# A fused attention, routed-expert and squared-gate kernel: raw weight loads are issued a step later in the attention

## The chip, the cores and the metric

The kernel runs on one core of a Trainium2 chip. The metric is the time of one execution on the device in microseconds (us). A core has TensorE (PE: matmuls, and PEld: its weight loads), VectorE (DVE), ScalarE (ACT), GpSimd (POOL) and SyncE (SP, which here only issues transfers and branches). Transfers run on the core's 16 DMA engines; SP, ACT and POOL issue them, each in the order of its own program.

## What is computed

Three layers, one behind the other. The first is attention over 4 batches, 8 heads, 576 positions and 64 features, with a causal window of 64 positions:

```
scores = scale * np.matmul(q, k.transpose(0, 1, 3, 2))
rel = pos[:, None] - pos[None, :]
mask = (rel >= 0) & (rel < window)          # window = 64
scores = np.where(mask, scores, -1000000000.0)
attn = softmax(scores)                       # written out in the reference
return np.matmul(attn, v).astype(np.float32)
```

Its output, 2304 rows of 512, goes through 8 experts (one expert for each row, chosen by the largest of 8 logits; rows with a negative skip score are left as they are): `h = relu(x @ w1[e])`, `y = gate * (h @ w2[e])`, added to x. The last layer is `h = x @ w_in`, a gate made of h and its square, and `g @ w_out`, with 2048 features inside.

## The kernel before

Everything is computed in float32 accuracy with pairs of rounded halves: a weight tile of 512 KB is loaded raw, ACT copies it into the high half (line 131), and another engine subtracts that half from the raw tile to get the low half (line 132). `split_pair` is that pair of operations, called a split here. The weights of the third layer come as 64-bit integers and are converted by DVE first (`convert_ops`).

**Raw places.** Raw tiles live in small pools: 4 places in one, 2 in another during the attention. `to_load` is the list of raw tiles in the order of their use. `load_raws` issues loads on SP as long as fewer than `most[0]` tiles are waiting and a place is free; `most[0]` is 2 + t // 2 in step t. `take_raw` gives a place up in the bookkeeping; a new tile in it still has to wait, in the program, until the split that read the old one has been done. So a load that is issued right behind a split waits, on SP, for that split's subtract.

**The attention.** The loop `for t in range(NT)` (line 578) has 18 steps, one for each 128 rows of the output, written as a pipeline of stages: step t does the scores of tile t (`stage_s`), the transposes of the probabilities of tile t - 2 (`stage_t`, named pt), and the product with the values of tile t - 3 (`stage_v`, named o, line 369), which is the first matmul of a step. So the first o product of the trace is step 3's, and the one at 65.61 us is step 11's. `stage_v` ends with two loads of values, vt, for the next block, into the halves that it has just read (`load_v`, line 299, on SP); they are read two steps later. In odd steps SP also issues q and k of a later block. ACT issues the store of the output tile x (line 387), which has two places. Every third step has routing work (`route_a`, `route_b`, `route_h` on POOL, `route_c`), which makes a number for each row by which the experts gather their rows.

At the end of a step stands one split, on ACT and POOL, if the raw tile has been known for two steps:

```
            if splits and since.get(splits[0][1:], t) + 2 <= t:
                work(splits, [pool])
            if t:
                load_raws()
```

`work` calls `do_split`, which calls `load_raws` itself behind the split. Beside it, from step 6 on, the operations of two conversions are spread over the steps (`convert_by_parts`), and this too calls `load_raws` when a conversion is done. Behind the loop comes the drain: the last stages, the last routing, and then the gathers for the first expert. In the experts and in the last layer splits, conversions and loads are called in other places, by the same functions.

Of the kernel before, what the change touches and what calls it, by code (L numbers as in the profile page):

```python
# [64 lines left out]
def moe_chain(  # L65
# [26 lines left out]
    pool, dve = nc.gpsimd, nc.vector  # L92
# [3 lines left out]
    def load_raws(eng=nc.sync):  # L96
        while to_load and len(raws) < most[0]:
            used = [n for _, n in raws.values()]

            last = to_load[0] in LATE  # L100
            room = [n for n in range(1 if last else len(rawp)) if used.count(n) < RAWS[n]]
            if not room:
                return
            u, c = to_load.pop(0)

            n = min(reversed(room), key=lambda n: left.get(n, 0))
            at = rawp[n]
            if u < U_IN:
                r = at.tile([P, 2, 512], F32, tag="raw", name=f"raw{u}_{c}")
                eng.dma_start(r, wu[u, :, c : c + 2])  # L110
            else:
                r = at.tile([P, 512, 2], I32, tag="raw", name=f"raw{u}_{c}")
                eng.dma_start(
                    r.rearrange("p n w -> p (n w)").bitcast(I64), wd[u - U_IN, :, c]
                )
            raws[u, c] = r, n
# [3 lines left out]
    def take_raw(key):  # L120
        r, n = raws.pop(key)
        left[n] = max(left.values(), default=0) + 1
        return r
# [5 lines left out]
    def split_pair(u, c, src, into, eng):  # L129
        t = into.tile([P, 2, 2, 512], F32R, tag="pair", name=f"w{u}_{c}")  # L130
        nc.scalar.activation(t[:, 0], src, AF.Copy)  # L131
        eng.tensor_tensor(t[:, 1], src, t[:, 0].bitcast(F32), ALU.subtract)  # L132
        halves[u, c] = t[:, :, 0]
        halves[u, c + 1] = t[:, :, 1]

    def convert_ops(w, r, mag=None):

        low, high = r[:, :, 0], r[:, :, 1]  # L140
        wf = w.bitcast(F32)
        v = nc.vector
        ops = [
            partial(
                v.tensor_scalar, w, high, 3, 0x3FFFFFFF, op0=ALU.logical_shift_left, op1=ALU.bitwise_and
            ),
            partial(
                v.scalar_tensor_tensor, w, high, -0x40000000, w, op0=ALU.bitwise_and, op1=ALU.bitwise_or
            ),
            partial(  # L150
                v.scalar_tensor_tensor, w, low, 29, w, op0=ALU.logical_shift_right, op1=ALU.bitwise_or
            ),
        ]
        if mag is None:
            ops.append(partial(v.tensor_single_scalar, high, high, 0x7FFFFFFF, ALU.bitwise_and))
            mag = high.bitcast(F32)
        ops.append(partial(v.scalar_tensor_tensor, wf, mag, LEAST, wf, op0=ALU.is_ge, op1=ALU.mult))
        return ops

    def convert(w, r):  # L160
        for op in convert_ops(w, r):
            op()

    def do_split(u, c, eng):
        split_pair(u, c, take_raw((u, c)) if u < U_IN else early.pop((u, c)), ring, eng)
        load_raws()

    def do_convert(u, c, into):
        if c % 2 == 0:
            early[u, c] = into.tile([P, 2, 512], F32, tag="early", name=f"c{u}_{c}")  # L170
        convert(early[u, c // 2 * 2][:, c % 2].bitcast(I32), take_raw((u, c)))
        load_raws()

    def convert_by_parts(todo, into):

        for _, u, c in todo:
            if c % 2 == 0:
                early[u, c] = into.tile([P, 2, 512], F32, tag="early", name=f"c{u}_{c}")
            for op in convert_ops(early[u, c // 2 * 2][:, c % 2].bitcast(I32), raws[u, c][0]):
                yield  # L180
                op()
            take_raw((u, c))
            load_raws()

    def work(todo, engines):

        for eng in engines[: len(todo)]:
            what, u, c = todo.pop(0)
            if what == "s":
                do_split(u, c, eng)  # L190
            else:
                do_convert(u, c, early_pool[0])
# [75 lines left out]
    with ExitStack() as actx:  # L268
# [40 lines left out]
        def scale_q(i):  # L309

            if i < NBLK:
                nc.scalar.activation(qt[i], qt[i], AF.Copy, scale=SCALE)
# [49 lines left out]
        def stage_v(t):  # L362
            o = psp.tile([P, H, P], F32, tag="o", name=f"o{t}")

            pts = [st.pop(("pt", 2 * t + k)) for k in range(2)]
            for h in range(H):
                for k in range(2):
                    half = (h + k) % 2
                    nc.tensor.matmul(  # L369
                        o[k * BLK : (k + 1) * BLK, h, 0:VW],  # L370
                        lhsT=pts[k][:, h // 2, half * BLK : (half + 1) * BLK],
                        rhs=vt[(2 * t + k) % B][:, h * VW : (h + 1) * VW],
                        start=True, stop=True,
                    )
            den = sm.tile([P, H, 1], F32, tag="den", name=f"den{t}")
            nc.vector.tensor_scalar_add(den, o[:, :, D : D + 1], 1e-9)
            rec = sm.tile([P, H, 1], F32, tag="rec", name=f"rec{t}")
            nc.vector.reciprocal(rec, den)
            x = ap2.tile([P, H, D], F32, tag="x", name=f"x{t}")
            nc.vector.tensor_tensor(x, o[:, :, 0:D], rec.to_broadcast([P, H, D]), ALU.mult)  # L380
            st["x", t] = x.rearrange("p h d -> p (h d)")
            i, b = divmod(2 * t, B)
            load_v(i + 1, b)
            load_v(i + 1, b + 1)
# [32 lines left out]
        def keep_warm(n):  # L417
            spare = psp.tile([P, P], F32, tag="o", name="spare")
            for _ in range(n):
                nc.tensor.matmul(spare, lhsT=ones, rhs=ones, start=True, stop=True)  # L420
# [108 lines left out]
        def route_c(t, n):  # L529

            ix = misc[:, 128 : 128 + NE * NT]

            last = t + n == NT
            near = not last and t + 2 * n >= NT
            for i in reversed(range(n)):
                to, at = st.pop(("to", t + i))
                nc.tensor.matmul(
                    ix, lhsT=to, rhs=at, start=(not last and i == n - 1), stop=(not near and i == 0)
                )
            if last:  # L540
                keep_warm(KEEP[2])
            if not near:
                nc.vector.tensor_tensor(idx if last else acc, ix, acc, ALU.add)
            if last:
                nc.vector.tensor_tensor(cnt_i, st.pop("cn"), base[:, 0], ALU.subtract)


        splits = [("s", p // 2, p % 2 * 2) for p in range(RING)]
# [27 lines left out]
        due, since = {}, {}  # L576
        parts = convert_by_parts(converts, earlyp)
        for t in range(NT):
            if t >= 3:
                stage_v(t - 3)  # L580
            if t >= 2:
                stage_t(t - 2)
            if t % 2:
                scale_q(t // 2 + 1)
            stage_s(t)
            most[0] = 2 + t // 2
            if t % 2:
                load_q(t // 2 + 2)
                load_k(t // 2 + 3)
            if t >= 3:  # L590
                store_t(t - 3, nc.scalar)
            if t >= 6:
                next(parts, None)
            if t >= 5:
                stage_l2(t - 5, *of[t - 5][1:])
            if t >= 4:
                stage_l(t - 4)
            if t >= 3:
                stage_x(t - 3)
            if t >= 5:  # L600
                t0, i, n, side = of[t - 5]
                if i == n - 1:
                    route_a(t0, n)
                    for f, l in (
                        (partial(route_b, t0, n, side), 1),
                        (partial(route_h, t0, n), 2),
                        (partial(route_c, t0, n), 4),
                    ):
                        due.setdefault(t + l, []).append(f)
            for f in due.pop(t, ()):  # L610
                f()
            if t >= 6:
                next(parts, None)

            if splits and since.get(splits[0][1:], t) + 2 <= t:
                work(splits, [pool])
            if t:
                load_raws()
            for key in raws:
                since.setdefault(key, t)  # L620

        t1, n = NT - ROUTES[-1], ROUTES[-1]
        t0 = t1 - ROUTES[-2]
# [33 lines left out]
        route_h(t1, n)  # L657
        route_c(t0, of[t0][2])
        route_c(t1, n)
        for _ in parts:  # L660
            pass
        work(splits, [pool] * len(splits))
# [445 lines left out]
```

## Time and profile before

| | |
|---|---|
| median of the runs shown | 731.54 us (731.29 to 736.42, 3 runs) |
| the profiled execution | 736.77 us, with a span of 735.0 us from the first to the last instruction |
| PE, PEld busy | 684.8 us (93%), 582.6 us (79%) |
| DVE, ACT, POOL busy | 431.6 us (59%), 382.9 us (52%), 94.6 us (13%) |
| mean granted TensorE clock | 0.975 of full speed |
| a split: copy on ACT, subtract on POOL | 1058 ns, 2360 ns (means) |
| loads of raw tiles | 62 of 512 KB from the experts' weights and 32 of the last layer's on SP |

The profile is of one execution. PE's busy time is that of pipelined matmuls, with modelled ends, so a busy PE can still be slow: the granted clock has two levels, 1.2 and 2.4 GHz, and a mean share below 1 says how much of a stretch ran at the lower. The loop of the attention ends at about 116 us, the drain at 145 us. The timeline gives for each group of instructions its start, its duration, engine, line, operation, tiles and, in brackets, the idle time in front of it with what ended it.

### The profile page before, as it was taken

How to read it: one execution, taken by the hardware profiler on the slowest of the kernel's cores; microseconds unless marked ns; L12 is line 12 of the kernel's file. 1: busy time of each engine (PE TensorE's matmuls, PEld its weight loads, DVE VectorE, ACT ScalarE, POOL GpSimd, SP SyncE). 2: the span in 40 equal slices, each digit the busy share in tenths (PEclk: the TensorE clock that was granted, in tenths of full speed). 3: DMA queues.
4: the chain of work that ended last, by engine and by line, in shares of the span. 5: the costliest groups of instructions: out<-in, count | busy, mean ns of one | idle time of the engine just before them, and what ended most of it. 6: DMA issues, size and time to landing. Idle time of an engine off the chain costs nothing.

```text
span 735.0 us, 12186 instructions
## 1 busy us (share of the span) xinstructions
PE 684.8 (93%) x4605; PEld 582.6 (79%) x4605; DVE 431.6 (59%) x852; ACT 382.9 (52%) x760; POOL 94.6 (13%) x96
## 2 busy tenths in 40 slices
PE   7987887798999999899999999999999999999997
PEld 6765666676777777488789899999989989999985
DVE  4678776458759268968788884434433333343332
ACT  5756561026556266456666665545444454455443
POOL 2336662402112112200000000000000000000000
PEclk9999998789999999999999999999999999999999
DMA  7998954248859349453233400303030020001002
GB/s 255 310 304 250 253 175 117 61 136 279 291 172 347 130 146 293 132 181 122 94 109 107 125 6 1 71 15 73 16 86 1 1 68 19 1 1 43 1 1 43
DMA packets 34502, 88.81 MB, mean 121 GB/s; under 512 B 6958, under 2 KB 8110, under 8 KB 34420
## 3 DMA queue, kind: packets, MB, share of 16 engines
q1 hardware_dynamic: 26352, 74.60, 33.5%
q10 hardware_dynamic: 5748, 6.57, 2.9%
q0 software_dynamic: 2320, 6.58, 2.9%
q8 instruction: 47, 0.77, 0.4%
q14 instruction: 35, 0.29, 0.1%
HBM read 75.65 MB, written 13.12 MB: 121 GB/s over the span
## 4 chain that ended last, share of the span: by engine, by line
PE 52%; DVE 4%; ACT 1%; DMA 1%; issue 1%; SPq 0%; ACTq 0%; DVEq 0%
PE h L865 25%; PE po L893 25%; PE p2x L855 1%; DVE c L886 1%; DMA x<-x 1%; DVE c_first L992 1%; DVE c L883 1%; ACT q L876 1%; DVE w L132 0%; DVE gs L884 0%; DVE q L875 0%; DVE x2T L127 0%; ACT q L872 0%; DVE q L879 0%; ACT part L902 0%
## 5 line engine op out<-in xcount | busy, mean ns | idle before, releaser
L865 PE MATMUL h<-x2T,w 128*128 128x384 f32 x1152 | 218.1, 337 | 1.0 <-DVE x2T L127 0.9
L893 PE MATMUL po<-w,gs 128*128 128x512 f32 x864 | 217.3, 395 | 1.6 <-ACT w L131 0.9
L865 PEld LDWEIGHTS h<-x2T,w 128*128 128x128 f32 x1152 | 204.6, 188 | 10.1 <-DVE x2T L127 1.7
L893 PEld LDWEIGHTS po<-w,gs 128*128 128x128 f32 x864 | 159.5, 188 | 32.2 <-ACT w L131 1.2
L872 ACT ACTIVATE q<-h 128x384 f32<-128x384 f32 x96 | 47.0, 490 | 108.4 <-PE h L865 106.8
L875 DVE TENSOR_SCALAR q<-q 128x384 f32<-128x384 f32 x96 | 34.3, 358 | 98.2 <-ACT q L872 98.1
L879 DVE TENSOR_TENSOR q<-hs,q 128x384 f32<-128x384 f32 x96 | 53.6, 559 | 49.8 <-ACT q L876 49.8
L881 ACT ACTIVATE gs<-q 128x384 fp32r<-128x384 f32 x96 | 50.4, 525 | 60.0 <-DVE q L879 60.0
L884 DVE TENSOR_TENSOR gs<-q,gs 128x384 fp32r<-128x384 f32 x96 | 53.6, 559 | 44.4 <-ACT gs L881 44.4
L131 ACT ACTIVATE w<-raw 128x1024 fp32r<-128x1024 f32 x64 | 65.3, 1058 | 19.1 <-PEq L808 6.4
L748 PE MATMUL y<-w,hT 128*128 128x512 f32 x264 | 70.9, 404 | 4.6 <-DVE hT L127 3.7
L748 PEld LDWEIGHTS y<-w,hT 128*128 128x128 f32 x264 | 47.4, 188 | 18.5 <-DVE hT L127 6.7
L876 ACT ACTIVATE q<-q 128x384 f32<-128x384 f32 x96 | 50.5, 526 | 22.0 <-DVE q L875 18.4
L132 DVE TENSOR_TENSOR w<-raw,w 128x1024 fp32r<-128x1024 f32 x50 | 59.0, 1220 | 3.9 <-ACT w L131 2.2
L343 ACT ACTIVATE pr<-s,nb 128x128 f32<-128x128 f32 x144 | 39.2, 383 | 23.0 <-DVE nb L339 23.0
L874 ACT ACTIVATE hs<-h 128x384 f32<-128x384 f32 x96 | 46.8, 488 | 0.0
L710 PE MATMUL ha<-w,mxT 128*128 128x512 f32 x132 | 35.5, 421 | 6.9 <-PEq L808 4.1
L132 POOL TENSOR_TENSOR w<-raw,w 128x1024 fp32r<-128x1024 f32 x14 | 33.0, 2360 | 57.7 <-ACT w L131 57.7
L710 PEld LDWEIGHTS ha<-w,mxT 128*128 128x128 f32 x132 | 25.7, 201 | 16.1 <-issue 9.5
L369 PE MATMUL o<-vt,pts 128*64 128x65 f32 x576 | 26.5, 247 | 9.5 <-DMA vt<-in_vs 8.0
L710 PE MATMUL hb<-w,mxT 128*128 128x512 f32 x132 | 35.2, 402 | 0.0
L127 DVE TENSOR_TENSOR hT<-hTp,hT 128x512 fp32r<-128x512 f32 x22 | 15.1, 688 | 32.4 <-ACT hT L126 27.2
(164 smaller groups left out, 708.9 us busy)
## 6 DMA issues: line engine op xcount, KB each, us to landing
raw<-in_wu SPq DMA_DIRECT2D x62, 512.0 KB, 5.3
raw<-in_wd SPq DMA_DIRECT2D x32, 512.0 KB, 3.8
x<-x SPq DMA_DIRECT2D x21, 256.0 KB, 3.7
vt<-in_vs SPq DMA_DIRECT2D x36, 130.0 KB, 6.3
x<-x ACTq DMA_DIRECT2D x18, 256.0 KB, 6.5
out<-out SPq DMA_DIRECT2D x36, 128.0 KB, 2.4
q<-in_qs SPq DMA_DIRECT2D x8, 512.0 KB, 5.7
kt<-in_ks SPq DMA_DIRECT2D x8, 512.0 KB, 6.4
```

Of the source, the lines that this page charges most:

```text
L131: nc.scalar.activation(t[:, 0], src, AF.Copy)
L132: eng.tensor_tensor(t[:, 1], src, t[:, 0].bitcast(F32), ALU.subtract)
L710: nc.tensor.matmul(ph, lhsT=xT[:, a, c, :], rhs=halves[4 * e + j, c][:, b, :], start=(n == 0), stop=(n == len(seq) - 1),)
L748: nc.tensor.matmul(py, lhsT=hT[j][:, a, c, :], rhs=halves[4 * e + 2 + j, c][:, b, :], start=(j == 0 and c == 0 and (a, b) == PASSES[0]), s ...
L865: nc.tensor.matmul(ph, lhsT=halves[U_IN + m // 4, c][:, b, (m % 4) * P : (m % 4 + 1) * P], rhs=xT[:, a, c, :], start=(n == 0), stop=(n == ...
L872: nc.scalar.activation(q, ph, AF.Relu, bias=0.5, scale=0.5)
L874: nc.scalar.activation(h, ph, AF.Copy)
L876: nc.scalar.activation(q, q, AF.Square)
L879: nc.vector.tensor_tensor(q, h, q, ALU.max)
L881: nc.scalar.activation(gs[:, 0], q, AF.Copy)
L884: dve.tensor_tensor(gs[:, 1], q, gs[:, 0].bitcast(F32), ALU.subtract)
L893: nc.tensor.matmul(po[i], lhsT=gs[:, a, i * P : (i + 1) * P], rhs=w[:, b, :], start=(m == m0 and (a, b) == PASSES[0]), stop=(m == m1 - 1 a ...
```

## The change

Two things. First, in the attention neither a split nor a conversion calls `load_raws` any more: a flag, `at_once`, is false until the drain's last statement, where it is set and `load_raws` is called once. From there on everything is called as before. Second, at the end of a step `load_raws` and the note in which step a tile came (`since`) now stand ahead of the split instead of behind it.

```diff
+    at_once = [False]
+
     def do_split(u, c, eng):
         split_pair(u, c, take_raw((u, c)) if u < U_IN else early.pop((u, c)), ring, eng)
-        load_raws()
+        if at_once[0]:
+            load_raws()
...
             take_raw((u, c))
-            load_raws()
+            if at_once[0]:
+                load_raws()
...
-            if splits and since.get(splits[0][1:], t) + 2 <= t:
-                work(splits, [pool])
             if t:
                 load_raws()
             for key in raws:
                 since.setdefault(key, t)
+
+            if splits and since.get(splits[0][1:], t) + 2 <= t:
+                work(splits, [pool])
...
         route_c(t1, n)
+        at_once[0] = True
+        load_raws()
         for _ in parts:
             pass
```

PE and DVE keep every instruction in its order. SP, ACT and POOL change in the attention and the drain alone. A raw tile is named by its unit and column (raw6_2), and w6_2 is its split; the last number is a running one. On SP from step 11's loads of q and k to the end of step 13, before:

```order
L290 DMA q7_1284<-in_qs 128x1024
L294 DMA kt_148<-in_ks 128x1024
L110 DMA raw6_2_1289<-in_wu 128x1024
L113 DMA raw32_2_1336<-in_wd 128x512
L299 DMA vt2_151<-in_vs 64x520
L299 DMA vt3_152<-in_vs 64x520
L113 DMA raw32_3_1441<-in_wd 128x512
L299 DMA vt0_149<-in_vs 64x520
L299 DMA vt1_150<-in_vs 64x520
L290 DMA q8_1517<-in_qs 128x1024
L110 DMA raw7_0_1554<-in_wu 128x1024
```

The same place in the changed kernel:

```order
L295 DMA q7_1277<-in_qs 128x1024
L299 DMA kt_148<-in_ks 128x1024
L110 DMA raw5_2_1324<-in_wu 128x1024
L110 DMA raw6_0_1326<-in_wu 128x1024
L304 DMA vt2_151<-in_vs 64x520
L304 DMA vt3_152<-in_vs 64x520
L110 DMA raw6_2_1431<-in_wu 128x1024
L304 DMA vt0_149<-in_vs 64x520
L304 DMA vt1_150<-in_vs 64x520
L295 DMA q8_1510<-in_qs 128x1024
L113 DMA raw32_2_1544<-in_wd 128x512
```

The pattern stays, two vt loads and one raw load for each step, but the raw tiles come later: raw6_2 moves from step 11 to 12, raw32_2 from step 11 to 13, raw7_0 from 13 to 15. The last of the attention, raw8_0, moves from step 16 to the end of the drain, behind the last store of x. Before, raw32_2 takes the place of raw4_0, which is split in the same step 11; now it takes the same place in step 13, and raw4_0 is split in step 12.

On ACT the splits' copies move one step: there is none in step 7, and the last, w6_2, moves from step 16 to step 17. The end of the loop on ACT, before (pr are the exponentials, x14 and gate9 stores of rows and gates, pts34 belongs to the drain):

```order
L456 ACTIVATE ex9_1886<-d9_1875 128x24
L131 ACTIVATE w6_2_1888<-raw6_2_1289 128x1024
L357 ACTIVATE pts30_1923<-pt30_1918 128x512
L343 ACTIVATE pr34_1956<-s34_1932,nb34_1952 128x128 x4
L343 ACTIVATE pr35_1961<-s35_1933,nb35_1954 128x128 x4
L387 DMA x1_68<-x14_1914 128x512
L507 DMA x1_68<-gate9_1995 128x3x1
L357 ACTIVATE pts34_2061<-pt34_2056 128x512
```

and in the changed kernel:

```order
L461 ACTIVATE ex9_1879<-d9_1868 128x24
L131 ACTIVATE w6_0_1883<-raw6_0_1326 128x1024
L362 ACTIVATE pts30_1916<-pt30_1911 128x512
L348 ACTIVATE pr34_1949<-s34_1925,nb34_1945 128x128 x4
L348 ACTIVATE pr35_1954<-s35_1926,nb35_1947 128x128 x4
L392 DMA x1_68<-x14_1907 128x512
L512 DMA x1_68<-gate9_1988 128x3x1
L131 ACTIVATE w6_2_2004<-raw6_2_1431 128x1024
L362 ACTIVATE pts34_2059<-pt34_2054 128x512
```

w6_2's copy now stands behind the gate's store and ahead of pts34. On POOL its subtract stands, as before, ahead of the six operations of `route_h` for rows 9 to 11, but it too is of step 17 now.

## Rows read from the trace of the kernel before

**Rows 1.** Stretches: duration, busy us (count) of each engine, clock, DMA share, GB/s.

```profile
16.00:44.00 28.00, 25.51 (x432) 19.80 (x428) 18.68 (x40) 20.32 (x54) 9.46 (x4) 0.95 1.03 313
65.60:87.00 21.40, 17.20 (x271) 13.18 (x271) 17.83 (x58) 13.99 (x35) 11.29 (x9) 0.92 0.88 266
```

**Rows 2.** PE's waits, 16 to 117: us in total, times, longest us.

```profile
PE o L369 <- DMA vt<-in_vs: 8.0, 7, 2.6
...
PE o L369 <- DVE oh L452: 1.4, 1, 1.4
...
PE px L393 <- DVE x L380: 0.6, 1, 0.6
```

**Rows 3.** PE's timeline: start, duration, instruction, count, [idle before it].

```profile
65.61 1.69 PE L369 MATMUL o<-vt,pts 128*64 128x65 f32 x32 [1.76 <-DMA vt<-in_vs]
67.23 1.97 PE L353 MATMUL pt<-ident,pr 128*128 128x128 f32 x8
...
74.69 1.16 PE L369 MATMUL o<-vt,pts 128*64 128x65 f32 x32
...
79.52 1.15 PE L369 MATMUL o<-vt,pts 128*64 128x65 f32 x32
80.61 1.09 PE L353 MATMUL pt<-ident,pr 128*128 128x128 f32 x8
...
87.06 0.33 PE L369 MATMUL o<-vt,pts 128*64 128x65 f32 x2 [2.63 <-DMA vt<-in_vs]
87.56 1.97 PE L369 MATMUL o<-vt,pts 128*64 128x65 f32 x30 [0.17 <-DMA vt<-in_vs]
89.45 1.66 PE L353 MATMUL pt<-ident,pr 128*128 128x128 f32 x8
...
106.09 0.33 PE L369 MATMUL o<-vt,pts 128*64 128x65 f32 x2 [0.92 <-DMA vt<-in_vs]
107.81 1.97 PE L369 MATMUL o<-vt,pts 128*64 128x65 f32 x30 [1.38 <-DVE oh L452]
109.70 1.77 PE L353 MATMUL pt<-ident,pr 128*128 128x128 f32 x8
```

**Rows 4.** Waits of SP's queue, 16 to 120: us in total, times, longest us.

```profile
SPq L110 <- POOL w L132: 20.3, 6, 8.0
SPq L113 <- POOL w L132: 14.0, 3, 4.9
...
SPq L299 <- DMA x<-x: 5.8, 3, 3.5
```

**Rows 5.** SP's timeline: start, duration of the issue, transfer, count.

```profile
58.78 1.11 SPq L299 DMA_DIRECT2D vt<-in_vs  x2
...
79.85 0.33 SPq L113 DMA_DIRECT2D raw<-in_wd  x1
80.27 1.13 SPq L299 DMA_DIRECT2D vt<-in_vs  x2
...
100.60 0.33 SPq L110 DMA_DIRECT2D raw<-in_wu  x1
101.03 1.11 SPq L299 DMA_DIRECT2D vt<-in_vs  x2
```

**Rows 6.** POOL's timeline, the subtract of step 11's split.

```profile
77.46 2.37 POOL L132 TENSOR_TENSOR w<-raw,w 128x1024 fp32r<-128x1024 f32 x1 [6.61 <-ACT w L131]
```

**Rows 7.** Issues, 16 to 117: transfer, count, KB each, median us to landing.

```profile
vt<-in_vs SPq DMA_DIRECT2D x30, 130.0 KB, 6.5
x<-x ACTq DMA_DIRECT2D x15, 256.0 KB, 8.7
```

**Rows 8.** Timelines of POOL, ACT and PE in the drain.

```profile
121.60 0.85 POOL L523 TENSOR_SCALAR at<-slot_c,rc,val 128x144 fp32r<-128x144 f32 x1
...
122.11 0.60 ACT L357 ACTIVATE pts<-pt 128x512 f32<-128x512 f32 x1 [6.16 <-PE o L369]
...
128.99 0.89 PE L537 MATMUL misc<-at,to 128*128 128x144 f32 x3 [1.10 <-DVE mine L439]
```

## The prediction

> **What bounds the kernel now.** I read the stretches first, then PE's waits, then PE's timeline step by step, then the SP queue and POOL. The change lies in the attention, the first 116.7 us of a 735.0 us span, with a drain behind it until the first expert starts. The later two thirds are TensorE work in which no instruction moves, so they only start earlier or later.
>
> In the attention PE should be the pace: a plain step, from one o product to the next, is 4.83 us (74.69 to 79.52 [rows 3]). But PE's longest wait there is for vt, the values of a block: 8.0 us in seven waits, and one more of 1.4 put down to DVE that is of the same kind, 9.4 in all [rows 2]. (I read the 1.4 as vt too: o does not use oh, and the pair's second DMA, issued half a microsecond behind the one at 101.03, would land about then.) Step by step: 1.76 us in step 11 (o at 65.61), 2.63 + 0.17 in step 14 (87.06, 87.56), 0.92 + 1.38 in step 17 (106.09, 107.81) [rows 3]; that is 6.86, and the other 2.5 lie in steps 6 and 8.
>
> Each of these three idle times is followed by slower matmuls. The eight transposes pt take 1.09 us at full clock (80.61), but 1.97, 1.66 and 1.77 behind the three stalls; o takes 1.15 (79.52), but 1.69 and twice 1.97 [rows 3]. In both stretches shown the mean granted clock is below 1: 0.95 and 0.92 [rows 1]. So a stall costs its idle time and then (0.54 + 0.88), (0.82 + 0.57) and (0.82 + 0.68) us in o and pt, 4.3 together; other instructions that fall into it I leave out.
>
> Why is vt late? A pair of vt loads may go out as soon as the o product that reads its place is done, and is needed two steps later. In step 12 that o ends at 74.69 + 1.16 = 75.85 [rows 3], but SP issues the pair at 80.27, right behind a raw load at 79.85 [rows 5]. That raw load wants the place that step 11's split gave up, and POOL's subtract of that split ends at 77.46 + 2.37 = 79.83 [rows 6]. SP works in order, so the pair sits 4.4 us behind a load that nobody needs yet. The same shows at 100.60 and 101.03 for step 17, and the pair at 58.78 for step 11 goes out behind three raw loads [rows 5]. Over the attention SP waits 20.3 + 14.0 us in nine such cases [rows 4].
>
> **The change part by part.** (1) The raw load moves out of the split. At the end of a step SP now asks for a place freed in an earlier step. Call L the time from the o product of a step to the end of that step's subtract. For step 12 the pair was held until L of step 11 had run out, one step after that o; now the wait for that subtract stands in front of step 13's pair, one whole step later. Step 11's subtract ends at 79.83, step 13's o at 79.52 + 1.15 = 80.67: the wait is over before the pair is released. At worst, where two plain steps follow each other and POOL has its six routing operations ahead of the subtract, I expect under 1 us of it to be left, and a pair has two plain steps less its o, 2 x 4.83 - 1.15 = 8.5 us, to land; the median landing is 6.5 [rows 7], so 2.0 us are in hand. The stalls of steps 14 and 17 then go: 2.80 + 2.30. For step 11, the pair stands behind one raw load that waits for a conversion, not three, so most of 1.76 goes; I take all of it and put the doubt into the deduction below. With the half-speed stretches behind them, 6.86 + 4.3 = 11.2 us.
>
> (2) Fewer raw bytes ahead. The splits from w2_0 on come one step later (no split in step 7, w6_2 in step 17), and each raw load behind them mostly two steps later. From 16 to 44 us the DMA engines are full (share 1.03, 313 GB/s [rows 1]), and the vt pair of step 8 stands behind one raw load fewer: 512 KB at 313 GB/s is 1.7 us. The stalls of steps 6 and 8 sum to 2.5; I take 1.7. Bounds: nothing, if what is ahead is replaced by something else, and 2.5 plus one more slow stretch of 1.4.
>
> The Trainium skill ("DMA: Bandwidth & Descriptors", Specifications) gives about 358 GB/s as what one core gets from HBM; the stretch at 313 agrees as an upper limit. By the page's figure 512 KB would be 1.5 us, and the sum would fall by 0.2.
>
> (3) What comes next in its place. From 65.6 to 87.0 the DMA engines are busy 0.88 of 21.4 us, 18.8 us of work [rows 1]. Without step 11's slow stretch (1.42) and step 14's idle (2.80) PE would want it done in 17.2. So up to 1.6 us comes back as later landings; nothing, if the slack from (2) covers it. The output tile x has two places and its store lands in 8.7 us at the median [rows 7] against 9.7 for two plain steps, so DVE and then the transposes of x can be held: PE has 0.6 of that now, once [rows 2]. I take 0.6 to 1.2. I deduct 2.9 in all: 1.6 for the DMA work, 0.9 for x, 0.4 for step 11.
>
> (4) The drain. w6_2's copy (ACT) and subtract (POOL) now stand at the end of step 17. ACT has 6.16 us idle in front of pts at 122.11, and the copy takes about 1 us. POOL's six routing operations end at 121.60 + 0.85 = 122.45; 2.4 us later is 124.8, and the product that reads them starts at 128.99, behind DVE [rows 8]. So nothing, with 4 us of cover on POOL; if the cover were gone, up to 2.4. raw8_0 moves behind the last x store on SP, where SP has only the read of the counts left. No cost.
>
> Sum: 11.2 + 1.7 - 2.9 = 10.0 us. The profiled execution took 736.77 us, 5.2 above the median of 731.54; I cannot see where those 5.2 lie. Since the mechanism is in the order of the program, I take the gain as it is: 736.8 - 10.0 = 726.8 for such an execution, **721.5 us** for the median. If part of the 5.2 were in these very stalls, the median would gain less.
>
> **The rivals.** A is the forecast: the three stalls behind raw loads go, a gain of 7.4 to 15.5 (15.1 is 11.2 + 2.5 + 1.4 without deduction), 716 to 724.1.
>
> B: the DMA engines take over. vt goes out earlier but lands later, since a cycle of three steps has about as many bytes as before, and part of the stalls returns with its slow stretches. For it: a share of 0.88 to 1.03 up to 87 us [rows 1], and vt pairs that already wait for an earlier store's completion, 5.8 us in three cases [rows 4]. Against: only 0.88 in the stretch with the 2.8 us stall, and every raw load stands later. If two of the three slow stretches stay (2.9) and a third of the idle time (2.3), the gain is 10.0 - 5.2 = 4.8: 726.7, with 725 to 731 around it. The Trainium skill ("DMA: Bandwidth & Descriptors", Issuing engines are not separate DMA queues) says that the sequencer's own time is usually small beside the DMA itself; taken alone that speaks for B, but here it is not the issue of 0.33 us that holds the pair, it is the wait in front of it.
>
> C, slower: nothing holds SP back any more, so vt pairs go out into a fuller queue and land late everywhere. It decides from a landing of 8.5 us on. At 11 us each two-step round is 2.5 short: in the three routing cycles from step 9 to 17, two rounds of each, 6 x 2.5 = 15 us of idle time, with a slow stretch of 1.4 for each cycle 19, against the 11.2 that go: 8 us slower, 739.5. Against it: raw loads in flight are limited by free places, and now fewer are in flight; the median is 6.5 [rows 7].
>
> D, the change does not do what it says: the subtract is so late that the raw load still holds the next pair. It needs L above two steps, 9.7 us and more, by as much as now. L is 79.83 - (65.61 + 1.69) = 12.5 for step 11, but the two steps behind it take 13.4 (o from 65.61 + 1.69 to 80.67). Then within 1 us of 731.5.
>
> **How the numbers follow.** A 0.62, B 0.28, C 0.04, D 0.06. One per cent of 731.5 is 7.3 us, about what a measurement of this kernel can tell from no change, so A is faster (0.62), B and D are within 1% (0.34), C is slower (0.04). The range 716.0 to 730.0 holds A, and of B and D most of B; it leaves out some 0.04 below, 0.12 above. For A alone 716 to 724.
>
> **What would show it.** In the changed kernel: SP's waits for POOL w fall from 34 us to little, or no longer stand ahead of a late vt pair; PE's wait for vt falls from 9.4 to under 3; pt stays near 1.1 us in steps 11, 14 and 17; the last o product of the loop starts about 10 us earlier; everything from the first expert on is shifted, not changed. I am wrong in (1) if vt pairs still go out 4 us behind their o, in (3) if they go out in time and PE still waits with DMA at 1.0 (B) or for x, and in (4) if the distance from the last o to the first gather grows.

## The result, and the profile after

The changed kernel takes 725.23 us (median of 4) beside 733.98 us of the kernel before (median of 4): ratio 0.9873, 95% interval 0.9824 to 0.9923. Run once more beside other kernels it gave 0.9877 (0.9836 to 0.9919). Single executions of one kernel lie up to 14 us apart, and as a rule those with a higher granted clock are the shorter ones, so small differences are read from many executions and not from one. Ratios and means leave out executions that were more than 1.5% above the kernel's shortest.

The profiled execution has a span of 723.6 us, 11.4 less than before. From TensorE's timeline, the starts of the o products:

| from … to | before, us | after, us | less by |
|---|---|---|---|
| step 3's o: start | 16.08 | 17.25 | -1.2 |
| step 3 to 9 | 36.92 | 33.31 | 3.6 |
| step 9 to 11 (ends with step 11's stall) | 12.61 | 10.84 | 1.8 |
| step 11 | 9.08 | 9.33 | -0.3 |
| step 12 | 4.83 | 6.08 | -1.3 |
| step 13 to 15 (step 14's stall) | 15.91 | 11.33 | 4.6 |
| step 15 to 17 | 10.66 | 9.67 | 1.0 |
| step 17 | 10.62 | 7.83 | 2.8 |
| first o of the drain to the first expert's transposes | 28.57 | 27.83 | 0.7 |
| from there to the end of the span | 589.7 | 590.1 | -0.4 |

So the gain is made in the attention, and the rest is shifted, not changed. The first row is no gain or loss of the change: up to there the instructions are the same. One profile stands behind each column, and single rows vary: in a second profile of the changed kernel (span 724.2 us) the first expert starts 9.4 us earlier than before, not 11.8. The attention of the profile before is not an unusual one: its first expert starts at 145.28 us, and that of the kernel below that changes the order alone, and gains nothing, at 146.09.

TensorE's waits after, 16 to 117 us (us in total, times, longest), as [rows 2]:

```profile
PE pt L358 <- DVE xT L400: 4.5, 6, 1.4
PE misc L542 <- DVE ls L419: 2.1, 2, 1.2
PE px L398 <- DVE x L385: 1.6, 3, 0.6
...
PE o L374 <- DMA vt<-in_vs: 0.5, 1, 0.5
```

The wait for values, 9.4 us before, is 0.5 us. What leads now are waits for DVE's copies (xT, ls), each 1.4 us or less. SyncE's queue, 16 to 120 us, as [rows 4]:

```profile
SPq L304 <- PE o L374: 15.8, 8, 5.5
SPq L110 <- POOL w L132: 10.9, 4, 4.6
SPq L113 <- POOL w L132: 5.7, 3, 2.6
```

The waits for POOL's subtract are halved, 34.3 to 16.6 us, not gone; but SyncE now waits most for the o product itself, which is when the pair of vt should go out. The timeline of steps 12 to 14, as [rows 5]:

```profile
72.76 1.11 SPq L304 DMA_DIRECT2D vt<-in_vs  x2
75.89 0.33 SPq L110 DMA_DIRECT2D raw<-in_wu  x1
77.99 1.12 SPq L304 DMA_DIRECT2D vt<-in_vs  x2
80.60 0.33 SPq L295 DMA_DIRECT2D q<-in_qs  x1
82.48 0.33 SPq L113 DMA_DIRECT2D raw<-in_wd  x1
82.92 1.40 SPq L304 DMA_DIRECT2D vt<-in_vs  x2
```

and TensorE's, as [rows 3]:

```profile
62.23 1.12 PE L374 MATMUL o<-vt,pts 128*64 128x65 f32 x30 [0.50 <-DMA vt<-in_vs]
64.53 1.09 PE L358 MATMUL pt<-ident,pr 128*128 128x128 f32 x8 [1.18 <-DVE xT L400]
...
69.54 0.53 PE L542 MATMUL misc<-at,to 128*128 128x144 f32 x3 [1.19 <-DVE ls L419]
70.54 0.18 PE L471 MATMUL misc<-oh,stri 128*128 128x27 bf16 x1 [0.47 <-DVE acc L548]
...
70.73 2.00 PE L374 MATMUL o<-vt,pts 128*64 128x65 f32 x32
72.67 1.49 PE L358 MATMUL pt<-ident,pr 128*128 128x128 f32 x8
...
76.81 1.15 PE L374 MATMUL o<-vt,pts 128*64 128x65 f32 x32
...
81.65 1.16 PE L374 MATMUL o<-vt,pts 128*64 128x65 f32 x32
82.73 1.09 PE L358 MATMUL pt<-ident,pr 128*128 128x128 f32 x8
...
97.81 1.15 PE L374 MATMUL o<-vt,pts 128*64 128x65 f32 x32
98.89 1.09 PE L358 MATMUL pt<-ident,pr 128*128 128x128 f32 x8
```

In step 12 the o product ends at 70.73 + 2.00 = 72.73 and its pair of vt goes out at 72.76; in step 13 at 77.96 and 77.99. Before, step 12's pair stood 4.4 us behind. Steps 14 and 17 (o at 81.65 and 97.81) have no stall and run o and pt at full speed. From step 4 to the end of the loop only step 12 has slow ones (2.00 and 1.49), behind step 11's waits. Of these, the ones for ls and acc stood there before too, and then step 12 ran at full speed; new in step 11 are 0.50 us for vt and 1.18 for xT. Before:

```profile
73.51 0.53 PE L537 MATMUL misc<-at,to 128*128 128x144 f32 x3 [1.09 <-DVE ls L414]
74.50 0.17 PE L466 MATMUL misc<-oh,stri 128*128 128x27 bf16 x1 [0.47 <-DVE acc L543]
```

The stretches and landings after, as [rows 1] and [rows 7]:

```profile
16.00:44.00 28.00, 26.51 (x488) 20.80 (x480) 18.92 (x41) 21.05 (x57) 9.48 (x4) 0.95 1.00 316
65.60:87.00 21.40, 19.30 (x320) 14.89 (x317) 18.00 (x55) 14.80 (x39) 13.68 (x10) 0.92 1.01 297
```

```profile
vt<-in_vs SPq DMA_DIRECT2D x32, 130.0 KB, 6.3
x<-x ACTq DMA_DIRECT2D x15, 256.0 KB, 7.3
```

The DMA engines are busier from 65.6 to 87 us (share 1.01, before 0.88), because the attention passes sooner, and the values land 6.3 us after issue at the median, as before. That median, like the 6.5 of [rows 7], is of few loads: the profile holds the landings of 8 of the 32 (5 of the 30 before). The second profile of the changed kernel has 28 of them, with a median of 6.9 and 9.0 us at the longest.

### The profile page after: what moved, and what is told of

Read it like the earlier page. It is cut to its first block, busy times and chain, and to the rows that moved or that the text cites. A ratio compares the mean times of both kernels' runs of the same rounds, so it can differ in the third digit from the quotient of the medians.

```text
span 723.6 us, 12188 instructions
## 1 busy us (share of the span) xinstructions
PE 678.7 (94%) x4605; PEld 578.4 (80%) x4605; DVE 430.5 (59%) x852; ACT 382.7 (53%) x760; POOL 93.6 (13%) x96
## 4 chain that ended last, share of the span: by engine, by line
PE 49%; DVE 7%; ACT 2%; issue 1%; DMA 0%; ACTq 0%; DVEq 0%; SPq 0%
PE po L901 24%; PE h L873 24%; DVE c L894 2%; ACT q L884 1%; PE p2x L863 1%; DVE gs L892 1%; DVE c L891 1%; DVE w L132 1%; DVE c_first L1000 1%; DVE q L883 1%; DVE q L887 1%; DVE x2T L127 0%; DMA x<-x 0%; ACT q L880 0%; PE spare L989 0%
## 5 line engine op out<-in xcount | busy, mean ns | idle before, releaser
L127 DVE TENSOR_TENSOR hT<-hTp,hT 128x512 fp32r<-128x512 f32 x22 | 15.1, 688 | 33.1 <-ACT hT L126 25.4
L344 DVE TENSOR_REDUCE nb<-s 128x4 f32<-128x512 f32 x36 | 23.1, 684 | 13.4 <-PE s L337 8.5
```

## The experiments

Three kernels stand around the change: is it the wait on SyncE, or the order of the bytes?

**The order alone.** From the kernel before:

```diff
-            if splits and since.get(splits[0][1:], t) + 2 <= t:
-                work(splits, [pool])
             if t:
                 load_raws()
             for key in raws:
                 since.setdefault(key, t)
+            if splits and since.get(splits[0][1:], t) + 2 <= t:
+                work(splits, [pool])
```

> The kernel before, with the raw load of the free places written ahead of the split, but the split and the conversion still load at once into the place they leave. On SP each raw load from the eighth step on now stands one pair of value tiles later than before, as it does after the change; but each one still needs the place of the split made in the same step, so SP still stops there. If the wait counts (the theory of the forecast): SP's idle time for POOL's w stays near the 34 us of before (25 to 40), the o product still waits for vt about three times, and the time is within 0.4% of before (ratio 0.996 to 1.004). If it is the order of the bytes on the DMA engines that counts (raw bytes behind the value tiles and not ahead of them): ratio 0.985 to 0.99, as after the change.

Measured: ratio 0.9997 (0.9968 to 1.0025). The waits, of TensorE and of SyncE's queue:

```profile
PE o L369 <- DMA vt<-in_vs: 9.0, 6, 2.3
```

```profile
SPq L110 <- POOL w L132: 29.2, 7, 8.8
SPq L113 <- POOL w L132: 7.6, 3, 4.9
```

36.8 us on SyncE and 9.0 on TensorE, as before. Later raw bytes alone bring nothing.

**A spare place.** From the kernel before, splits and loads where they were:

```diff
-            most[0] = 2 + t // 2
+            most[0] = min(2 + t // 2, 5)
...
         route_c(t1, n)
+        most[0] = 1 + NT // 2
+        load_raws()
```

> The kernel before, split and loads in their old places, but at most five of the raw places are filled in the attention loop, so that a place stays spare and a load that follows a split takes the place left by an earlier one. If the wait counts: SP's idle time for POOL's w falls under 15 us, the o product's waits for vt are gone (under 2 us in place of 8.0), and the ratio is 0.985 to 0.99, as after the change. If the step's place in the code (the raw load beside the branch, one step later) is what counts, and not the wait: ratio 0.996 to 1.004.

Measured: 0.9885 (0.9849 to 0.9922). The same two views:

```profile
PE o L369 <- DMA vt<-in_vs: 1.8, 2, 1.4
```

```profile
SPq L113 <- POOL w L132: 7.8, 3, 3.1
...
SPq L110 <- POOL w L132: 5.3, 3, 1.9
```

With the calls where they were, the gain comes once the wait falls (13.1 us). What the change moved is one way to it, not the thing itself.

**Another queue.** From the kernel before, with a flag, `on_pool`, that is true around the loop's split alone:

```diff
     def do_split(u, c, eng):
         ...
-        load_raws()
+        load_raws(pool if on_pool[0] else nc.sync)
```

> The kernel before, but in the attention loop the raw load that follows a split is issued by POOL, which has just made the split, and no longer by SP. The load goes out at the same moment as before, with the same bytes ahead of the same value tiles; only SP no longer stops for it. If the wait on SP counts: the o product's waits for vt go from 8.0 us to under 2.5, the half-clock stretches at steps 11, 14 and 17 go, and the ratio is 0.985 to 0.992 (a little less gain than after the change, by the 1.7 us that the raw bytes ahead of step 8's value tiles cost and what POOL spends to issue). If the DMA engines and not the queue hold the value tiles (rival B, or the order of the bytes): ratio 0.995 to 1.003. If issuing from POOL itself is dear: POOL is late with the next w and the ratio is above 1.0.

Measured: 0.991 (0.9879 to 0.9942).

```profile
PE o L371 <- DMA vt<-in_vs: 0.6, 2, 0.4
```

```profile
SPq L110 <- POOL w L132: 4.1, 1, 4.1
```

Up to 51 us the raw loads go out 3 to 8 us later than before, but from 57 to 90 us within 1 us of their old times (79.65, 87.14 and 90.40 us; before 79.85, 86.42 and 89.68), and the waits for vt of steps 14 and 17 are gone all the same. They also go over another DMA queue here, so this run alone doesn't tell SyncE's wait from the place of the raw bytes ahead of the values in one queue; the spare place does, where they stay on SyncE's. The three together show that the cause was the in-order wait on SyncE. The Trainium skill ("DMA: Bandwidth & Descriptors", Issuing engines are not separate DMA queues) says that issuing on several engines saves only the sequencer's time, usually small beside the DMA; for the 0.33 us of an issue that holds here, but not for a wait in front of it, which cost about 1% of this kernel.

**Filling the wait.** Is it TensorE's waiting that brings the half-clock stretches behind it? From the kernel before:

```diff
             if t >= 3:
+                if t in (11, 14, 17):
+                    keep_warm({11: 24, 14: 36, 17: 14}[t])
                 stage_v(t - 3)
```

> The kernel before, with idle-time matmuls of ones (results unused) ahead of the o product in steps 11, 14 and 17: 24, 36 and 14 of them, which at 62 ns each fill 1.5, 2.25 and 0.87 us of the 1.76, 2.63 and 0.92 us that TensorE waits there for value tiles. The waits for POOL on SP and the arrival of the value tiles stay as they are. If TensorE's waiting is what brings the half-clock stretches behind it (the forecast's 4.3 us of its 11.2): the granted clock at 66.8, 87.3 and 107.7 us is no longer half, the o and pt of these steps run at 1.15 and 1.1 us again, and the time falls by 2.5 to 4.3 us (ratio 0.994 to 0.997). If the stretches come whatever TensorE does there: ratio 0.999 to 1.003 and the stretches stand where they stood.

Measured: 1.006 (1.0024 to 1.0095), slower, where 0.994 to 0.997 was expected. Yet in its profile the three slow stretches are gone (pt of steps 11, 14 and 17 takes 1.09 us, at a granted clock of 1.00) and the first expert starts at 138.03 us, 7.2 before its old place; then the experts and the last layer take 596.5 us instead of 589.7. That difference stands in TensorE's waits at the branches for second tiles (136 to 290 us), first of the kernel before, then of this one:

```profile
PE ha L710 <- PEq L808: 4.1, 2, 2.8
```

```profile
PE ha L712 <- PEq L810: 11.4, 5, 3.9
```

The wait is of TensorE's own sequencer, behind the branch; the 74 matmuls and their weight loads had made the program in front longer. The clock fell there too: from the first expert to 290 us it is 0.96 here and 0.98 before, while up to the first expert it is 0.95 and 0.91. So the next kernel has as many instructions as before; `keep_warm_wide` issues matmuls of 512 columns, with the same ones:

```diff
-                    keep_warm({11: 24, 14: 36, 17: 14}[t])
+                    keep_warm_wide({11: 7, 14: 10, 17: 4}[t])
...
-        for _ in range(WARM):
+        for _ in range(WARM - 28):
             nc.tensor.matmul(warm, lhsT=ones, rhs=ones, start=True, stop=True)
+        keep_warm_wide(7)
```

> The kernel before with TensorE's waits for value tiles filled as in the run with the idle-time matmuls, but with matmuls of 512 columns (7, 10 and 4 of them, results unused, about the same 1.5, 2.2 and 0.9 us), and 28 of the 58 warm-up matmuls ahead of the attention put together to 7 wide ones, so that TensorE has just as many instructions as before and the code behind the attention lies where it lay. That run ended its attention 7.2 us earlier than the kernel before, and lost 6.8 us in the experts, where TensorE's sequencer stood idle at the branches for second tiles for 11.4 us in place of 4.1. If that loss came from where the added code put the branches: the first expert starts at 138 to 140 us as there, the experts take the 590 us of before, and the time is 4 to 7 us less than before (ratio 0.990 to 0.995). If the loss comes from the attention's end being moved at all, or the half-clock stretches only went elsewhere: ratio 0.998 to 1.006.

Measured: 0.9984 (0.995 to 1.0019). The sequencer's wait is back at its old size:

```profile
PE ha L719 <- PEq L817: 4.3, 2, 3.0
```

and the three stretches that ran at half clock before (columns as in [rows 1], the clock is the third number from the end), first before, then here:

```profile
66.80:70.20 3.40, 3.40 (x24) 2.38 (x24) 3.01 (x14) 2.71 (x4) 1.72 (x1) 0.50 0.96 350
87.30:90.70 3.40, 3.23 (x38) 3.05 (x37) 1.06 (x3) 0.03 (x1) 2.35 (x1) 0.51 0.92 245
107.70:111.10 3.40, 3.29 (x37) 3.20 (x38) 1.06 (x4) 0.45 (x2) 2.36 (x1) 0.50 0.79 203
```

```profile
66.80:70.20 3.40, 3.14 (x52) 2.07 (x50) 3.17 (x8) 2.53 (x6) 2.37 (x1) 1.00 0.78 274
87.30:90.70 3.40, 3.40 (x55) 2.34 (x53) 2.54 (x5) 1.01 (x3) 1.46 (x1) 1.00 0.97 206
107.70:111.10 3.40, 2.77 (x49) 2.10 (x50) 2.46 (x6) 1.58 (x7) 0.00 (x0) 1.00 0.93 246
```

All three are at 2.4 GHz. But step 12, which ran at full speed before, now has a slow o and pt:

```profile
72.20 1.67 PE L369 MATMUL o<-vt,pts 128*64 128x65 f32 x32
73.80 1.97 PE L353 MATMUL pt<-ident,pr 128*128 128x128 f32 x8
```

So two of the three stretches went, and one came a step later. And the gain of 4 to 7 us did not come, though this profile's first expert starts at 140.42 us, 4.9 before its old place: the interval allows at most 3.7 and none at all. Each execution's span and mean granted clock say what became of it. Take span x (1 - clock) as the time not granted: 17.4 us over 21 executions of the kernel before, 13.6 over 12 of this one, 3.8 less (standard error 1.5). The remainder of the span grew from 716.6 to 718.7 us, by 2.1 (standard error 1.1). So filling brings part of the clock back, and about half of that seems to be paid for again by the fill itself, presumably where the values come before it ends. The run before this one does not show it in its executions: 16.8 us not granted over 11, beside 16.2 over 16 of the kernel before. That its loss in the experts came from where the longer code put the branches is what the pair suggests; an earlier end of the attention alone does not bring it, since the kernel after, whose first expert starts earlier still, waits 4.0 us there. What exactly the sequencer waits for isn't settled.

**What comes next after the change.** Now from the kernel after; first that kernel itself, once more:

> The changed kernel once more, beside the others on the same chip: ratio 0.985 to 0.991 to the kernel before, 724 to 727 us.

Measured: 0.9877 (0.9836 to 0.9919).

```diff
             for f in due.pop(t, ()):
                 f()
-            if t >= 6:
+            if t >= 6 and t != 9:
                 next(parts, None)
```

> The kernel after, with the conversion's eighth of ten DVE operations moved from the end of step 9 to the beginning of step 10's group (the ninth and tenth follow one place later), so that it no longer stands beside POOL's subtract. If DVE, held 1.5 us by that subtract, took the place of the value tiles in step 11 (the term of the forecast that did not come): the operation takes 0.7 us in place of 2.2, TensorE's waits for xT and ls around 62 to 70 us fall by 1 to 2 us, the half-clock stretch at 70 us goes, and the time is 1 to 3 us under the kernel after (ratio to before 0.983 to 0.987). If DVE's lateness there has other causes or another wait stands right behind it: the ratio is that of the kernel after within 0.1%.

Measured: 0.9871 (0.9825 to 0.9917), no difference to the kernel after that these six executions can resolve; the 1 to 3 us expected are within the interval. The rows tell why there is little to see. DVE's operation and POOL's subtract at that place, in the profile after, in the second one of the same kernel, and here:

```profile
61.46 2.22 DVE L185 SCALAR_TENSOR_TENSOR c<-raw,c 128x512 int32<-128x512 int32 x1
...
60.78 2.35 POOL L132 TENSOR_TENSOR w<-raw,w 128x1024 fp32r<-128x1024 f32 x1
```

```profile
63.62 0.69 DVE L185 SCALAR_TENSOR_TENSOR c<-raw,c 128x512 int32<-128x512 int32 x1
...
60.57 2.35 POOL L132 TENSOR_TENSOR w<-raw,w 128x1024 fp32r<-128x1024 f32 x1
```

```profile
61.27 1.70 DVE L185 SCALAR_TENSOR_TENSOR c<-raw,c 128x512 int32<-128x512 int32 x1
...
64.63 0.68 DVE L185 SCALAR_TENSOR_TENSOR c<-raw,c 128x512 int32<-128x512 int32 x1
...
60.07 2.34 POOL L132 TENSOR_TENSOR w<-raw,w 128x1024 fp32r<-128x1024 f32 x1
```

Where the subtract is under way when DVE's operation comes, DVE ends 0.55 us after the subtract (63.68 against 63.13; 62.97 against 62.41); where it is over, DVE takes 0.69. In the kernel after it met the operation in one profile and not in the other, and step 11 took 9.33 us in the one and 7.84 in the other. Of these 1.5 us, 0.8 is o and its wait for vt; pt's wait for xT is 1.18 in the one and 0.50 in the other, so the collision can account for 0.7. The edit moved every operation from there on by one place, and so put the one in front, the seventh, beside the subtract. No run here took the collision away.

```diff
-            x = ap2.tile([P, H, D], F32, tag="x", name=f"x{t}")
+            x = ap2.tile([P, H, D], F32, tag="x", name=f"x{t}", bufs=3)
```

> The kernel after, with three places for the tile x in place of two, so that the DVE multiply that writes it no longer waits for the store of two steps earlier. DVE's waits for the x store (4.9 us in three places after the change) go to nothing. If they are on the path (the forecast's deduction of 0.9 us): TensorE's waits for x (1.6 us) and xT (4.5 us) fall, and the time is 0.5 to 2 us under the kernel after (ratio to before 0.984 to 0.987). If DVE only waits while TensorE has other work: no difference to the kernel after that can be measured.

Measured: 0.9897 (0.9847 to 0.9948), no gain, though DVE's wait for the store is gone from its waits. Its span without the time not granted is 708.9 us, 3.2 under the kernel after in the same series (712.1), but 15.3 us were not granted, against 10.7. So whatever three places save shows only in the remainder, and as much was lost in the clock; in its profile o waits 2.3 us for vt again.

The last two were run in another series, as was the run with the wide matmuls, on another chip and beside the kernel before alone (median there 736.97 us), so they compare with the kernel after by their ratios only:

```diff
-            most[0] = 2 + t // 2
+            most[0] = min(2 + t // 2, 5)
...
         at_once[0] = True
+        most[0] = 1 + NT // 2
         load_raws()
```

> The kernel after, and at most five raw places filled in the attention loop, so that a raw load finds a place left a step or more earlier. SP's idle time for POOL's w, 16 us after the change (one pair of loads near 49 us waits 5 us ahead of step 10's value tiles), falls under 8 us, and the wait of step 10's o product for vt (0.5 to 1.7 us) goes. If what is left of the wait is worth anything: 0.5 to 2.5 us under the kernel after, ratio to before 0.984 to 0.987. If value tiles wait for the DMA engines there, or DVE is next in line: the same as the kernel after within 0.1%.

Measured: 0.9922 (0.9889 to 0.9955). SyncE's waits for w are down to 0.4 us and o's for vt to 0.6, and the time is no better than after the change. (What was expected took two waits for one: the 0.5 us is that of step 11's o, whose pair stood behind the two loads near 49 us; the 1.7 us of the second profile is that of step 10's, whose pair went out ahead of them.) With all three edits together:

> The kernel after with the three further edits together: a spare raw place, a third place for x, the conversion's eighth operation one place later. Each alone did little (the second and third alone: 0.9897 and 0.9871, beside 0.9877 of the kernel after). If each only uncovers the next wait, together they give 1 to 4 us more than the kernel after: ratio to before 0.982 to 0.987. If the steps are bound by their own work by now: 0.986 to 0.990.

Measured: 0.989 (0.9851 to 0.9928). In its profile two operations of the conversion met a subtract (2.32 and 2.33 us). None of these runs is measurably faster than the changed kernel; a gain of up to some 3 us would not show. The waits that the change left on SyncE (16.6 us) cost nothing that these runs can measure.

## Why the prediction was right, step by step

**The mechanism** was right: a raw load that nobody needed yet held the values behind it. The vt pair goes out with its o, PE's wait for vt falls from 9.4 us to 0.5 (to 3.0 in the second profile, just at the limit that was set), and everything from the first expert on is shifted by 11.8 us (145.28 to 133.47; by 9.4 in the second profile) without a change of its own. Two signs came less clearly than forecast: SyncE's waits for POOL fell by half and not to little, and the last o product of the loop starts 8.3 us earlier, not about 10.

**(1) The three stalls with their slow stretches, 11.2 us.** In the profile, steps 9 to 12 and 13 to the drain give 1.8 - 0.3 + 4.6 + 1.0 + 2.8 = 9.9, in the second profile 7.3. In the first, step 11's slow stretch (1.42) went, but 0.50 us for vt and 1.18 for xT came in its place; its pair had gone out behind two raw loads, not one. The split between idle time and clock was mis-sized. In the series in which the changed kernel was run once more, on one chip, the mean span went from 732.0 us (16 executions) to 722.8 (5), by 9.2; the time not granted went from 16.2 to 10.7, so up to 5.5 of it is clock and 3.7 the rest, where the forecast had 4.3 of clock in 10.0. It had counted only o and pt behind three stalls, and left out by its own words whatever else fell into a stretch. That the clock falls behind such a stall and stays up when it is filled, the fill runs show for these three places; they also show that a stretch can come a step later instead.

**(2) Fewer raw bytes, 1.7 us.** Steps 6 to 9 took 21.34 us before, 18.33 and 18.53 in the two profiles after: 2.9 less, between the value taken and the upper bound (3.9). How much of it are bytes is not shown: the kernel that issues the raw loads from POOL has 19.68, without SyncE's wait for a split, but up to 51 us its raw loads go out later too. One profile each. Full DMA engines don't move a steady number of bytes either: 313 GB/s is the mean of 28 us, and single stretches of 5 us have up to 368 before (16 to 21 us) and 387 after (71 to 76), so the figure that the prediction takes as an upper limit is one for the mean only.

**(3) The deduction, 2.9 us.** Near in size, and its reasons hold in part. Against the 11.2 of (1), the first profile lacks 1.3 and gives back 1.3 in step 12; the second lacks 3.9. The DMA engines did fill up (share 1.01). In the first profile o waits 0.5 us for vt, but in the second 3.0. There the pair that step 10 reads went out at 47.94, 2.4 us behind step 8's o, landed only at 56.92, and o waited for it:

```profile
47.94 1.11 SPq L304 DMA_DIRECT2D vt<-in_vs  x2
```

```profile
56.97 2.35 PE L374 MATMUL o<-vt,pts 128*64 128x65 f32 x32 [1.68 <-DMA vt<-in_vs]
```

The store of x costs nothing that three places for x visibly win back. What the deduction did not have is DVE: in step 11 pt waits for xT behind the operation that POOL's subtract held. That operation was held before too, while TensorE waited for vt, so the change laid the wait bare and did not make it. Its price is not measured, and why the slow stretch then comes in step 12 stays open.

**(4) The drain, nothing.** It is 0.7 us shorter, in the second profile 0.5 longer. The added split ends at 107.50 + 2.35 = 109.85, well before the routing product at 117.36, which still waits for DVE as in [rows 8]:

```profile
107.50 2.35 POOL L132 TENSOR_TENSOR w<-raw,w 128x1024 fp32r<-128x1024 f32 x1 [4.39 <-ACT w L131]
...
117.36 0.89 PE L542 MATMUL misc<-at,to 128*128 128x144 f32 x3 [1.09 <-DVE mine L444]
```

**The sum and the base.** 10.0 us were forecast; the profiles differ by 11.4 and 10.8, the medians by 8.8, and the mean spans above by 9.2. The predicted 721.5 is 3.7 below 725.2, and A's own upper end of 724.1 is passed by 1. Of the 3.7, 2.4 are the base: 731.54 was a median of three, and the kernel's medians beside the others were 733.1 to 734.8 on one chip and 737.0 on another; the other 1.2 are the gain. The 5.2 us between 731.54 and the profiled 736.77, which the prediction could not place, are within the spread of single executions. (A's largest gain of 15.5 is 0.4 more than the 15.1 that it adds up; nothing hangs on it.)

**The rivals.** B had its premise, DMA engines at 1.0, and a little of its conclusion, the late pairs of the second profile; but the stalls of steps 14 and 17 returned in neither. By its time alone the result lies in B's 725 to 731 and outside A's 716 to 724.1; that is the low base, and what decides for A are the waits and the gain of 8.8 against B's 4.8. So it was the width of the stated range that held the time. C did not come: values land in 6.3 and 6.9 us at the median. D is refuted for the change, but it is just what the order alone shows: with the load behind the same step's split, nothing is gained.

## What to carry to other kernels

A queue that issues in order makes each transfer wait for the oldest unmet wait in it, so a prefetch whose buffer isn't free yet belongs behind whatever is needed soon, or on another queue, or needs a spare buffer; all three gave about the same here, and moving it without freeing it sooner gave nothing. Price a stall by its idle time and by the slower matmuls behind it, but don't expect to buy all of the second part back by filling. Once the first wait is gone, small waits of another engine carry the rest, and the spread of single executions hides what each is worth.

## What the runs showed of the hardware

- Behind each of three idle times of 1.8 to 2.8 us (step 17's in two pieces) TensorE's granted clock was 0.50, that is 1.2 GHz; with the idle time filled by matmuls it was 1.00 in the same places, though in one of the two runs a slow stretch then stood in step 12 (pt 1.97 us). Executions of one kernel differ with it: after the change from 720.0 us of span at a clock of 0.989 to 723.6 at 0.982.
- A DVE operation with two inputs in SBUF stood still while POOL's subtract ran: 2.22 us in place of 0.69, ending 0.55 us behind it; before the change too (2.20, from 63.90, with a subtract from 63.21 to 65.55). The Trainium skill ("SBUF — State Buffer", SBUF: two separate sides) says that the two share a port pair as an exclusive lock, so that who comes second fully blocks, also for a DVE operation with two SBUF inputs against a GpSimd one that reads SBUF; the rows agree.
- With 74 matmuls added in the attention, TensorE's sequencer waited 11.4 us instead of 4.1 behind branches 55 to 190 us later; with the old number of instructions it was 4.3, and 3.9 to 4.5 in every other profile here. What it waits for is not shown.
